# Two-phase units in the first MoE layer of a fused attention and two-MoE kernel, and a few splits on other engines

## Chip, core and metric

The kernel runs on one core of a Trainium2 chip. The metric is device time in microseconds (us), of which the median of three runs is taken. The engines of the core are named as in the profile: PE (TensorE, the matmuls), DVE (VectorE), ACT (ScalarE), POOL (GpSimd) and SP (SyncE, which issues all the DMAs here). Each engine works through its own instructions strictly in the order of the program; semaphores tie the engines together.

## What is computed

Three layers, one after the other, all in fp32:

```python
# attention, 4 batches x 8 heads, 576 positions, head size 64, block-causal mask of 64
attn = softmax(mask(q @ k.T / 8));  x = concat_heads(attn @ v)          # x: 2304 x 512
# first MoE layer (one dense expert of 2048 hidden units)
h = x @ w_in;  g = h * cos(h);  x = g @ w_out                           # 2304 x 512
# second MoE layer: 8 experts of 1024 hidden units, a gate balanced by 8 rounds
logits = x @ w_gate;  P = exp(logits - logits.max())
for _ in range(8): P /= P.sum(1); P /= P.sum(0); P *= N / E
out = sum over e of P[:, e:e+1] * (max(x @ w1[e], 0) @ w2[e])           # out: 2304 x 512
```

`w_in` and `w_out` arrive as 64-bit floats; the kernel takes the two 32-bit words of each and builds the fp32 number from them with integer operations ("conversions" below).

## The kernel before

**Split products.** A matmul takes operands of the type fp32r. To come near fp32, each operand is split into a high part (a copy into fp32r) and a low part (the operand minus its high part), and a product is three matmuls (`mm3`, L521 to L524): high by high, high by low, low by high. So for each operand some engine makes a copy (nearly always ACT) and some engine a subtraction (DVE or POOL).

**First MoE layer** (`moe1`, L710 to L916). Tokens are taken in three blocks of 768 and hidden units in 16 slices of 128. One pair of them is a unit: 48 units, `n` = 0 to 47, block by block; units 0 to 15 are called group 1 here, 16 to 31 group 2, 32 to 47 group 3. In PE's order a unit is: `hidden` for its first 384 tokens (12 matmuls), `hidden` for its other 384 tokens (12), and then `o_part` (L766) of the unit before, in two halves of 12 matmuls. `hidden` writes into one of two PSUM buffers, so a unit's first half needs the buffer that the unit before has read for the last time in `times`. Between the two lies the elementwise chain of a half: `ki` (an integer multiple of two pi, L740 on ACT or L742 on DVE), `r` (L744, DVE), the sine (L749, ACT), `times` (g = h * sine, L753, DVE), the high part of g (`g_hi`, L757, ACT), the low part (`g_lo`, L761, DVE). The weights of a unit are split as well: part 0 (`w_in`) for `hidden`, part 1 (`w_out`) for `o_part`: `w_hi` (L723, ACT) and `w_lo` (L728, POOL or DVE); `wsplit` does both and does nothing where they are there already.

In group 1, `unit` (L808) also carries the conversions of those weight tiles that attention has not converted, up to two in a unit: `magnitude` and `rounding` on ACT (L102, L109), `clamp`, `shift` and `bits` on DVE (L114, L118, L125), `add` on POOL (L131), which is issued in the unit after, and `fetch`, the load of the tile three places on (L90, SP). The order in `unit` before is: first half up to the sine, then the other half's `ki` between steps of the first, and so on: the halves alternate, and each engine's steps for the two halves are interleaved with the weights' splits and the conversions. Three split tiles are made in attention and kept in spare columns of `xh` and `xl`, so units 0 and 1 split fewer weights. In unit 1 the two halves of `hidden` are written into two of the six banks (`a11`, `a12`) that `o_part` accumulates in. Other work is hung between the units by number: `steps` (the gate's `gate_prep` L542, the gate's logits, the first expert weights), `leftover` (the end of attention, L512 to L515) and `tprep` (sums of token blocks for the second layer, one step a unit, L913).

**Second MoE layer** (L1010 to L1091). 96 groups `g` (three token blocks by 8 experts by 4 quarters of an expert) of seven products with sums of blocks in the manner of Strassen and Winograd, and six products `y` (L982) with `w2`, each added into `oa` by DVE (L1006; L1000 or L998 in the first groups). While group `g` runs, the weights of `g + 1` are prepared: the sums (`sums`, L599 to L602, POOL), high and low parts of `w1` (`hi_b` ACT, `lo_b` DVE L613 and L615) and of its sums (`hi_a` L621 ACT, `lo_a` L624 DVE, 1024 columns), and `v` for `w2` (L632 ACT, L633 POOL, twice). `open_group` of the next group needs `lo_a` at its ninth matmul. In groups 1 to 5 the gate's rounds run in between at places that `plan` (L965) names (`gate`): small products on PE and a chain of eight short steps on DVE (L956 to L959, L947 to L951).

Of the kernel before, what the change touches and what calls it, by code (L numbers as in the profile page):

```python
# [10 lines left out]
F32 = mybir.dt.float32  # L11
# [32 lines left out]
def attention_moe_kernel(ctx: ExitStack, tc: tile.TileContext, qk, v, w_a, gate, w_b, out):  # L44
# [107 lines left out]
    def attention():  # L152
        with tc.tile_pool(name="at1", bufs=1) as p1, tc.tile_pool(name="at2", bufs=2) as p2, \
# [355 lines left out]
            e = NH - 2  # L509
            n = F1 + 1  # L510
            more = [(tla[:, 0:DM], odd_sums[0][:, 0:DM]), (tt[0][:, 0:DM], RAW[1][:, 0:DM])]
# [5 lines left out]
    with tc.manual_schedule():  # L517
# [192 lines left out]
        def moe1():  # L710
            nonlocal th, tl
            with tc.tile_pool(name="m1", bufs=2) as p:
# [22 lines left out]

                def reduce_h(ps, by_act=False):
                    ki = p.tile([128, TB], I32, tag="ki", name="ki", bufs=1)
                    r = p.tile([128, TB], F32, tag="r", name="r")
                    if by_act:
                        nc.scalar.activation(ki, ps, AF.Identity, bias=quarter, scale=float(1 / TWO_PI))  # L740
                    else:
                        nc.vector.tensor_scalar(out=ki, in0=ps, scalar1=float(1 / TWO_PI), scalar2=0.25,  # L742
                                                op0=ALU.mult, op1=ALU.add)
                    nc.vector.scalar_tensor_tensor(out=r, in0=ki, scalar=float(-TWO_PI), in1=ps,  # L744
                                                   op0=ALU.mult, op1=ALU.add)
                    return r

                def sine(r):
                    nc.scalar.activation(r, r, AF.Sin, bias=half_pi)  # L749
# [42 lines left out]
                for j, unit in enumerate(FIRST):  # L792
                    wj[unit] = SPARE[j]
                last = NU - F1

                FIRST_HALF, FRAMES = NH // 4, 14
                w3 = p.tile([128, 4 * HK], F32, tag="s", name="w3", bufs=1).bitcast(I32)
                todo = list(range(FIRST_HALF, NHALF))
                share = [((n + 1) * len(todo) + FRAMES - 1) // FRAMES - (n * len(todo) + FRAMES - 1) // FRAMES
                         for n in range(FRAMES)]  # L800
                adds = []
# [6 lines left out]
                def unit(n):  # L808
                    t0 = units[n][0] * HB
                    w = wj.pop((n, 0))  # L810
                    ks = [todo.pop(0) for _ in range(share[n])] if n < FRAMES else []
                    own = [pbank.tile([128, 512], F32, tag=t, name="h")[:, 0:TB] if n == 1 else None
                           for t in ("a11", "a12")]
                    pa = hidden(*w, t0, own[0])
                    ra = reduce_h(pa, True)
                    if (n, 1) not in wj:
                        w_hi(n, 1)
                        w_lo(n, 1)
                    for k in adds:
                        conv.add(k)  # L820
                    adds[:] = ks
                    sine(ra)
                    pb = hidden(*w, t0 + TB, own[1])
                    new = (n + 1, 0) not in wj
                    if new:
                        w_hi(n + 1, 0)
                    ga = times(pa, ra)
                    if new:
                        w_lo(n + 1, 0, nc.vector)
                    rb = reduce_h(pb, True)  # L830
                    g_hi(n, 0, ga)
                    g_lo(n, 0, ga)
                    sine(rb)
                    for k in ks[0:1]:
                        conv.magnitude(k, more[k % 2][0])
                    gb = times(pb, rb)
                    g_hi(n, 1, gb)
                    g_lo(n, 1, gb)
                    for k in ks[1:2]:
                        conv.magnitude(k, more[k % 2][0])  # L840
                    for k in ks:
                        conv.rounding(k, more[k % 2][1])
                    for k in ks:
                        conv.clamp(k)
                        conv.shift(k)
                        conv.bits(k)
                        fetch(k + 3)
# [7 lines left out]
                for blk in range(N // HB - 1):  # L855
                    for i, k in ((2 if blk else 9, 2 * blk), (5 if blk else 11, 2 * blk + 1)):
                        at = (blk + 1) * F1 + i - last
                        steps.setdefault(at, []).append(lambda k=k: logits(k, psh, "h"))
                        steps.setdefault(at + 1, []).append(lambda k=k: logits_t(k, psh, "h"))
                steps[12 - last] = [gate_prep]  # L860
                tgen = None
                fetch(FIRST_HALF + 1)
                fetch(FIRST_HALF + 2)
                for n in range(NU + 1):
                    if n == F1 + 10:
                        th = post.tile([128, 3, 2, TB], F32R, tag="th", name="th", bufs=1)
                        tl = post.tile([128, 3, 2, TB], F32R, tag="tl", name="tl", bufs=1)
                        tgen = tprep(0, nc.vector)
# [5 lines left out]
                    elif n < NU:  # L874
# [5 lines left out]
                        ra = reduce_h(pa)  # L880
                        pb = hidden(*w, t0 + TB)
                        sine(ra)
                        wsplit(n + 1, 0)
# [24 lines left out]
                    if n:  # L908
# [3 lines left out]
                        wj.pop((n - 1, 1))  # L912
                    if tgen:  # L913
                        next(tgen, None)
# [38 lines left out]
        def cols(more):  # L953
# [7 lines left out]
            if more:  # L961
                rows()

        col = lambda i: lambda: cols(i < SK_ITERS - 1)
        plan = {(0, "S3"): first_logits, (0, "S4"): last_logits, (1, "A12"): gmax, (1, "y0"): start_p,  # L965
                (1, "y4"): col(0), (5, "A12"): col(SK_ITERS - 1)}
# [15 lines left out]
        def y(g, t):  # L982
# [13 lines left out]
            if tb == 0 and e == 0:  # L996
                if j == 0:
                    nc.scalar.activation(o, acc, AF.Copy)  # L998
                else:
                    nc.vector.tensor_tensor(out=o, in0=acc, in1=o, op=ALU.add)  # L1000
            elif e == 0 and j == 0:
                nc.vector.tensor_scalar(out=o, in0=acc, scalar1=p, scalar2=None, op0=ALU.mult)
            else:
                if tb == 0 and e == 1 and j == 0:
                    nc.vector.tensor_scalar(out=o, in0=o, scalar1=P[:, row, 0:1], scalar2=None, op0=ALU.mult)
                nc.vector.scalar_tensor_tensor(out=o, in0=acc, scalar=p, in1=o, op0=ALU.mult, op1=ALU.add)  # L1006
# [4 lines left out]
        for g in range(NG + 1):  # L1011
# [21 lines left out]
            def gate(at):  # L1033
                if (g, at) in plan:
                    plan[g, at]()

            if now:
# [6 lines left out]
                if g:  # L1044
                    nc.scalar.activation(c[0], x, AF.Copy)  # L1045
                    if w:
                        w.sums(fin)
                        w.hi_b()
                    product(g, x, "S2", "T2", False)
                    nc.scalar.activation(c[1], x, AF.Copy)  # L1050
                splits("T2")
                z = psz.tile([128, TB], F32, tag="z", name="hz")
# [17 lines left out]
            if now:  # L1070
# [6 lines left out]
                nc.vector.tensor_tensor(out=c[1], in0=yy, in1=c[1], op=ALU.add)  # L1077
                hidden_block(g, 1, c[1])
                wload(g + 2)
            ys(2)  # L1080
            if w and g:
                w.lo_a()
            ys(3)
            if w:
                w.v(0)
            ys(4)
            gate("y4")
            if w:
                w.v(1)
# [32 lines left out]
```

## Time and profile before

| | |
|---|---|
| median of 3 runs | 2142.88 us (2142.86 to 2143.22) |
| the profiled execution, its own time | 2142.92 us |
| its span, first to last instruction | 2141.1 us |
| PE busy | 2120.3 us (99%) |
| weight loads of PE | 1892.6 us (88%) |
| DVE busy | 1476.5 us (69%) |
| ACT busy | 979.1 us (46%) |
| POOL busy | 885.4 us (41%) |
| attention | about 0 to 189 us |
| first MoE layer | about 189 to 617 us |
| second MoE layer | about 613 to 2141 us |

Durations below come from the profiled execution. 1.82 us of its own time lie outside its span. The ends of matmuls are modelled in the profile, so that PE's idle time is shown too small; the starts are not, and lost time on PE is read here from start to start.

### The profile page before, as it was taken

Reading aid. Unit: us, or ns where it says so; the run is one execution under the profiler, and the core shown is the slowest. Engines: PE = TensorE matmul, PEld = TensorE weight load, DVE = VectorE, ACT = ScalarE, POOL = GpSimd, SP = SyncE. Lnnn points to the kernel's source line nnn. Section 1 sums busy time; section 2 is a strip of 40 time slices with the busy share of each in tenths; the row PEclk is TensorE's granted clock in tenths of the full one; section 3 lists DMA queues with packets and bytes.
Section 4 is the critical chain, followed back from the end, with each engine's and each line's share of the span. In section 5 each row is a group of like instructions: output and inputs, shape, how many; then the busy total and the mean of one; then the engine's idle time right before and its main releaser. Section 6 shows DMA issues by size and latency. Waiting matters only on the chain.

```text
span 2141.1 us, 29753 instructions
## 1 busy us (share of the span) xinstructions
PE 2120.3 (99%) x10959; PEld 1892.6 (88%) x10959; DVE 1476.5 (69%) x2409; ACT 979.1 (46%) x1846; POOL 885.4 (41%) x801
## 2 busy tenths in 40 slices
PE   9999999999999999999999999999999999999999
PEld 7887989998988888889888898888988889888898
DVE  7886886566668766666776666666777666666665
ACT  7887665344454333433443333443434433344342
POOL 4544433333323434335544343433654334343341
PEclk9999999999999999999999999999999999999999
DMA  6775320001011212112113121221212212122120
GB/s 169 184 188 141 98 72 1 7 1 40 1 40 60 79 60 71 68 60 79 60 60 109 60 79 60 71 68 60 79 60 99 69 60 79 60 71 68 60 79 30
DMA packets 77185, 152.84 MB, mean 71 GB/s; under 512 B 33232, under 2 KB 36816, under 8 KB 77040
## 3 DMA queue, kind: packets, MB, share of 16 engines
q1 hardware_dynamic: 77040, 150.95, 22.7%
q8 instruction: 86, 1.41, 0.3%
q14 instruction: 59, 0.48, 0.1%
HBM read 136.91 MB, written 4.87 MB: 66 GB/s over the span
## 4 chain that ended last, share of the span: by engine, by line
PE 84%; DVE 7%; issue 5%; POOL 2%; ACT 2%; DMA 0%; POOLq 0%; ACTq 0%; DVEq 0%
PE acc L522 12%; PE acc L524 12%; PE acc L523 12%; PE hx L524 6%; PE hx L522 6%; PE hx L523 6%; PE o L358 4%; PE acc L777 3%; PE hy L524 3%; PE hy L522 3%; PE hy L523 3%; POOL jl L728 2%; PE hz L524 2%; PE hz L523 2%; PE hz L522 2%
## 5 line engine op out<-in xcount | busy, mean ns | idle before, releaser
L633 POOL TENSOR_TENSOR wv<-stg,wv 128x512 fp32r<-128x512 f32 x190 | 333.7, 1777 | 853.9 <-ACT wv L632 853.9
L522 PE MATMUL acc<-wv,hh 128*128 128x512 f32 x1152 | 457.0, 397 | 0.0
L524 PE MATMUL acc<-wv,hl 128*128 128x512 f32 x1152 | 455.8, 396 | 0.0
L523 PE MATMUL acc<-wv,hh 128*128 128x512 f32 x1152 | 454.7, 395 | 0.0
L1006 DVE SCALAR_TENSOR_TENSOR oa<-acc,P,oa 128x512 f32<-128x512 f32 x540 | 378.9, 740 | 4.9 <-PE acc L524 4.3
L977 ACT ACTIVATE hh<-c 128x384 fp32r<-128x384 f32 x288 | 151.2, 525 | 407.1 <-DVE c L1062 167.1
L978 DVE SCALAR_TENSOR_TENSOR hl<-c,hh 128x384 fp32r<-128x384 f32 x288 | 163.9, 569 | 176.0 <-ACT hh L977 176.0
L524 PEld LDWEIGHTS acc<-wv,hl 128*128 128x128 f32 x1152 | 216.3, 188 | 53.5
L523 PEld LDWEIGHTS acc<-wv,hh 128*128 128x128 f32 x1152 | 216.1, 188 | 43.5
L522 PEld LDWEIGHTS acc<-wv,hh 128*128 128x128 f32 x1152 | 216.4, 188 | 42.6
L728 POOL TENSOR_TENSOR jl<-raw,jh 128x512 fp32r<-128x512 f32 x78 | 111.1, 1425 | 270.8 <-ACT jh L723 260.5
L1055 DVE TENSOR_TENSOR c<-hz,c 128x384 f32<-128x384 f32 x96 | 53.4, 556 | 191.2 <-PE hz L524 191.2
L1045 ACT ACTIVATE c<-hx 128x384 f32<-128x384 f32 x95 | 46.9, 493 | 275.5 <-PE hx L524 275.5
L624 DVE TENSOR_TENSOR wal<-s,wah 128x1024 fp32r<-128x1024 f32 x96 | 171.5, 1787 | 0.0
L749 ACT ACTIVATE r<-r,half_pi 128x384 f32<-128x384 f32 x96 | 59.3, 617 | 162.5 <-DVE r L744 162.2
L524 PE MATMUL hy<-xh,wal 128*128 128x384 f32 x384 | 128.9, 336 | 1.0 <-DVE wal L624 1.0
L522 PE MATMUL hx<-th,wah 128*128 128x384 f32 x384 | 128.8, 335 | 0.6 <-ACT c L1045 0.6
L522 PE MATMUL h<-xh,jh 128*128 128x384 f32 x368 | 125.0, 340 | 4.2 <-DVE g L753 4.2
L522 PE MATMUL hy<-xh,wah 128*128 128x384 f32 x384 | 128.7, 335 | 0.4 <-DVE c L1062 0.2
L524 PE MATMUL hx<-th,wal 128*128 128x384 f32 x384 | 128.6, 335 | 0.0
L523 PE MATMUL hy<-xl,wah 128*128 128x384 f32 x384 | 128.4, 334 | 0.0
L523 PE MATMUL hx<-tl,wah 128*128 128x384 f32 x384 | 128.4, 334 | 0.0
(246 smaller groups left out, 4874.2 us busy)
## 6 DMA issues: line engine op xcount, KB each, us to landing
stg<-in_w_b_dram SPq DMA_DIRECT2D x192, 512.0 KB
st<-in_qk_dram SPq DMA_DIRECT2D x64, 144.0 KB
cw<-in_w_a_dram SPq DMA_DIRECT2D x17, 512.0 KB
v<-in_v_dram SPq DMA_DIRECT2D x31, 160.0 KB
tt<-inv SPq DMA_DIRECT2D x32, 144.0 KB
out_dram<-oa SPq DMA_DIRECT2D x18, 256.0 KB
kb<-qb SPq DMA_DIRECT2D x31, 144.0 KB
qb<-qa SPq DMA_DIRECT2D x31, 144.0 KB
```

The lines of the kernel that those rows point to most:

```text
L358: nc.tensor.matmul(o[:, q0:q1], vt[:, c], e, start=c == 0, stop=True, skip_group_check=c > 0)
L522: nc.tensor.matmul(ps, lh, rh, start=first, stop=False, skip_group_check=go_on)
L523: nc.tensor.matmul(ps, lh, rl, start=False, stop=False, skip_group_check=go_on)
L524: nc.tensor.matmul(ps, ll, rh, start=False, stop=last, skip_group_check=go_on)
L624: eng.tensor_tensor(out=self.al, in0=self.s, in1=self.ah.bitcast(F32), op=ALU.subtract)
L633: eng.tensor_tensor(out=t[:, DM:2 * DM], in0=src, in1=t[:, 0:DM].bitcast(F32), op=ALU.subtract)
L728: eng.tensor_tensor(out=lo, in0=raw[units[n][1]][:, part * DM:(part + 1) * DM], in1=hi.bitcast(F32), op=ALU.subtract)
L749: nc.scalar.activation(r, r, AF.Sin, bias=half_pi)
L777: nc.tensor.matmul(acc[half, b][:, at:at + w_], w[:, s], h[:, t0:t0 + w_], start=f == 0 and i == 0 and at == 0, stop=f == F1 - 1 and i == ...
L977: nc.scalar.activation(hh, src, AF.Relu)
L978: nc.vector.scalar_tensor_tensor(out=hl, in0=src, scalar=0.0, in1=hh.bitcast(F32), op0=ALU.max, op1=ALU.subtract)
L1006: nc.vector.scalar_tensor_tensor(out=o, in0=acc, scalar=p, in1=o, op0=ALU.mult, op1=ALU.add)
```

## The change

- `unit` in group 1 becomes two-phase: both halves of `hidden` are issued, then each elementwise step for both halves, before the next step. `ki` is always made by ACT there and is written into the buffer of `r`. The conversions' steps are gathered at the end in the same manner. The low part of a unit's `w_out` (`w_lo(n, 1)`) goes from POOL to DVE; POOL keeps the `add`s.
- The conversions are shared out differently: none in unit 0, the last in unit 13 as before.
- `gate_prep` goes from unit 12 to unit 21; `leftover` and `tprep` begin one unit later; `tprep` makes no step at unit 32.
- In units 17 and 33 the next unit's weights are split ahead of the sine.
- Second layer: `lo_a` runs on POOL in groups 1 to 5 and in the last group of a token block (31 and 63); the splits of `w2` for group 1 go from group 0 into group 1; `last_logits` goes behind the last sum of group 0; the six first multiplications by `P` (L1005) go from DVE to ACT.

```diff
-            n = F1 + 1
+            n = F1 + 2
...
-                    if by_act:
-                        nc.scalar.activation(ki, ps, AF.Identity, bias=quarter, scale=float(1 / TWO_PI))
...
-                FIRST_HALF, FRAMES = NH // 4, 14
+                FIRST_HALF = NH // 4
...
+                share = [0, 2, 2, 2, 1, 2, 2, 1] + [2] * 6
...
-                    pa = hidden(*w, t0, own[0])
-                    ra = reduce_h(pa, True)
-                    if (n, 1) not in wj:
-                        w_hi(n, 1)
-                        w_lo(n, 1)
+                    one, two = (n, 1) not in wj, (n + 1, 0) not in wj
+                    hs = [hidden(*w, t0 + i * TB, own[i]) for i in range(2)]
+                    r = [p.tile([128, TB], F32, tag="r", name="r") for _ in range(2)]
+                    for a, b in zip(r, hs):
+                        nc.scalar.activation(a.bitcast(I32), b, AF.Identity, bias=quarter, scale=float(1 / TWO_PI))
                     for k in adds:
                         conv.add(k)
                     adds[:] = ks
-                    sine(ra)
-                    pb = hidden(*w, t0 + TB, own[1])
-                    new = (n + 1, 0) not in wj
-                    if new:
+                    for a, b in zip(r, hs):
+                        nc.vector.scalar_tensor_tensor(out=a, in0=a.bitcast(I32), scalar=float(-TWO_PI), in1=b,
+                                                       op0=ALU.mult, op1=ALU.add)
+                    for a in r:
+                        sine(a)
+                    if two:
                         w_hi(n + 1, 0)
-                    ga = times(pa, ra)
-                    if new:
+                    g = [times(b, a) for a, b in zip(r, hs)]
+                    if two:
                         w_lo(n + 1, 0, nc.vector)
-                    rb = reduce_h(pb, True)
-                    g_hi(n, 0, ga)
-                    g_lo(n, 0, ga)
-                    sine(rb)
-                    for k in ks[0:1]:
-                        conv.magnitude(k, more[k % 2][0])
-                    gb = times(pb, rb)
-                    g_hi(n, 1, gb)
-                    g_lo(n, 1, gb)
-                    for k in ks[1:2]:
+                    for i in range(2):
+                        g_hi(n, i, g[i])
+                    if one:
+                        w_hi(n, 1)
+                    for i in range(2):
+                        g_lo(n, i, g[i])
+                    if one:
+                        w_lo(n, 1, nc.vector)
+                    for k in ks:
                         conv.magnitude(k, more[k % 2][0])
                     for k in ks:
                         conv.rounding(k, more[k % 2][1])
                     for k in ks:
                         conv.clamp(k)
                         conv.shift(k)
+                    for k in ks:
                         conv.bits(k)
                         fetch(k + 3)
...
-                steps[12 - last] = [gate_prep]
+                steps[F1 + 5 - last] = [gate_prep]
...
-                    if n == F1 + 10:
+                    if n == F1 + 11:
...
                         pb = hidden(*w, t0 + TB)
+                        if units[n][1] == 1:
+                            wsplit(n + 1, 0)
                         sine(ra)
...
-                    if tgen:
+                    if tgen and n % F1:
                         next(tgen, None)
...
-        plan = {(0, "S3"): first_logits, (0, "S4"): last_logits, (1, "A12"): gmax, (1, "y0"): start_p,
+        plan = {(0, "S3"): first_logits, (0, "c1"): last_logits, (1, "A12"): gmax, (1, "y0"): start_p,
...
                 if tb == 0 and e == 1 and j == 0:
-                    nc.vector.tensor_scalar(out=o, in0=o, scalar1=P[:, row, 0:1], scalar2=None, op0=ALU.mult)
+                    nc.scalar.activation(o, o, AF.Copy, scale=P[:, row, 0:1])
...
                     nc.scalar.activation(c[1], x, AF.Copy)
+                    if g == 1:
+                        Weights(1).v(0)
+                        Weights(1).v(1)
...
                 hidden_block(g, 1, c[1])
+                gate("c1")
                 wload(g + 2)
...
             if w and g:
-                w.lo_a()
+                w.lo_a(nc.gpsimd if g < 6 or left == 1 else nc.vector)
             ys(3)
-            if w:
+            if w and g:
                 w.v(0)
             ys(4)
             gate("y4")
-            if w:
+            if w and g:
                 w.v(1)
```

## Rows read from the trace of the kernel before

**Rows 1.** Busy by stage: from:to, length, PE, PEld, DVE, ACT, POOL, clock, DMA, GB/s.
```profile
189.38:217.65 28.27, 24.12 (x123) 22.17 (x122) 18.42 (x32) 19.78 (x35) 10.07 (x8) 0.88 0.42 123
217.65:267.93 50.28, 50.28 (x289) 47.12 (x288) 42.20 (x70) 34.65 (x65) 23.13 (x16) 1.00 0.32 104
267.93:334.66 66.73, 61.62 (x337) 56.09 (x336) 52.33 (x88) 41.71 (x78) 23.63 (x17) 0.97 0.18 57
334.66:612.73 278.07, 276.57 (x1581) 255.13 (x1580) 180.31 (x316) 121.85 (x222) 93.48 (x66) 1.00 0.04 13
627.97:728.34 100.37, 98.25 (x490) 86.46 (x489) 80.15 (x166) 43.44 (x83) 39.68 (x38) 1.00 0.19 64
646.02:678.30 32.28, 32.28 (x165) 29.05 (x164) 26.82 (x60) 13.53 (x27) 12.72 (x13) 1.00 0.19 66
728.34:1121.34 393.00, 393.00 (x1951) 351.83 (x1950) 266.24 (x404) 159.13 (x304) 176.24 (x159) 1.00 0.21 68
1121.34:1137.70 16.36, 16.02 (x79) 14.05 (x78) 12.00 (x18) 6.25 (x12) 8.00 (x8) 1.00 0.32 111
```

**Rows 2.** What PE waited for: us in total, times, longest us.
```profile
PE h L522 <- DVE g L753: 4.2, 4, 3.1
...
PE hy L524 <- DVE wal L624: 1.0, 3, 0.3
PE h L524 <- POOL jl L728: 1.0, 2, 0.6
...
PE pcs L955 <- DVE sm L951: 0.8, 1, 0.8
PE hx L522 <- ACT c L1045: 0.6, 1, 0.6
```

**Rows 3.** PE in order of time, unit 1: start, us, line, [idle before <-releaser].
```profile
203.62 0.58 PE L777 MATMUL acc<-hh,xh 128*128 128x256 f32 x1 [3.32 <-DVE g L753]
```

**Rows 4.** ACT in order of time, unit 0: ahead of the first sine.
```profile
192.50 1.28 ACT L749 ACT_TABLE_LOAD   x1
```

**Rows 5.** DVE in order of time, a unit with two conversions.
```profile
266.14 0.56 DVE L753 TENSOR_TENSOR g<-h,r 128x384 f32<-128x384 f32 x1 [0.68 <-ACT r L749]
...
271.65 0.69 DVE L125 SCALAR_TENSOR_TENSOR raw<-w,tla 128x512 int32<-128x512 int32 x1
...
273.18 1.71 DVE L125 SCALAR_TENSOR_TENSOR raw<-cw,tt 128x512 int32<-128x512 int32 x1
...
276.04 0.56 DVE L753 TENSOR_TENSOR g<-h,r 128x384 f32<-128x384 f32 x1 [0.69 <-ACT r L749]
```

**Rows 6.** POOL in order of time, the same unit.
```profile
273.05 1.30 POOL L728 TENSOR_TENSOR jl<-raw,jh 128x512 fp32r<-128x512 f32 x1 [5.64 <-ACT jh L723]
```

**Rows 7.** SP's queue in order of time: the issue of a weight load.
```profile
221.02 0.33 SPq L90 DMA_DIRECT2D w<-in_w_a_dram  x1
```

**Rows 8.** Busy time by stage, the us in which that load has landed.
```profile
225.50:226.50 1.00, 1.00 (x8) 0.91 (x7) 0.90 (x2) 0.61 (x2) 0.01 (x1) 1.00 0.00 0
```

**Rows 9.** PE in order of time, the first matmul of unit 34.
```profile
490.79 0.41 PE L522 MATMUL h<-xh,jh 128*128 128x384 f32 x1 [0.36 <-DVE g L753]
```

**Rows 10.** DVE in order of time, a subtraction beside a POOL operation.
```profile
1028.47 2.52 DVE L70 TENSOR_TENSOR xl<-tt,xh 128x768 fp32r<-128x768 f32 x1
```

**Rows 11.** POOL in order of time, that operation.
```profile
1028.34 1.84 POOL L645 TENSOR_TENSOR tt<-xh,tt 128x768 f32<-128x768 f32 x1
```

**Rows 12.** ACT in order of time, group 3 of the experts.
```profile
670.80 1.04 ACT L621 ACTIVATE wah<-s 128x1024 fp32r<-128x1024 f32 x1
```

**Rows 13.** DVE in order of time, the same group: a round of the gate.
```profile
672.43 0.31 DVE L959 TENSOR_TENSOR P<-P,sm 128x144 f32<-128x144 f32 x1
...
673.96 0.44 DVE L951 TENSOR_REDUCE sm<-P 128x8 f32<-128x144 f32 x1
674.32 0.68 DVE L1000 TENSOR_TENSOR oa<-acc,oa 128x512 f32<-128x512 f32 x1
...
677.66 1.87 DVE L624 TENSOR_TENSOR wal<-s,wah 128x1024 fp32r<-128x1024 f32 x1
```

More of the change, by code (lines that the diff above doesn't have):

```diff
@@ L734, in wsplit, with reduce_h @@
                         w_lo(n, part)
-                def reduce_h(ps, by_act=False):
+                def reduce_h(ps):
                     ki = p.tile([128, TB], I32, tag="ki", name="ki", bufs=1)
                     r = p.tile([128, TB], F32, tag="r", name="r")
-                    if by_act:
-                        nc.scalar.activation(ki, ps, AF.Identity, bias=quarter, scale=float(1 / TWO_PI))
-                    else:
-                        nc.vector.tensor_scalar(out=ki, in0=ps, scalar1=float(1 / TWO_PI), scalar2=0.25,
-                                                op0=ALU.mult, op1=ALU.add)
+                    nc.vector.tensor_scalar(out=ki, in0=ps, scalar1=float(1 / TWO_PI), scalar2=0.25,
+                                            op0=ALU.mult, op1=ALU.add)
                     nc.vector.scalar_tensor_tensor(out=r, in0=ki, scalar=float(-TWO_PI), in1=ps,
@@ L794, in moe1 @@
                 last = NU - F1
-                FIRST_HALF, FRAMES = NH // 4, 14
+                FIRST_HALF = NH // 4
                 w3 = p.tile([128, 4 * HK], F32, tag="s", name="w3", bufs=1).bitcast(I32)
                 todo = list(range(FIRST_HALF, NHALF))
-                share = [((n + 1) * len(todo) + FRAMES - 1) // FRAMES - (n * len(todo) + FRAMES - 1) // FRAMES
-                         for n in range(FRAMES)]
+                share = [0, 2, 2, 2, 1, 2, 2, 1] + [2] * 6
                 adds = []
@@ L810, in unit @@
                     w = wj.pop((n, 0))
-                    ks = [todo.pop(0) for _ in range(share[n])] if n < FRAMES else []
+                    ks = [todo.pop(0) for _ in range(share[n])] if n < len(share) else []
                     own = [pbank.tile([128, 512], F32, tag=t, name="h")[:, 0:TB] if n == 1 else None
                            for t in ("a11", "a12")]
-                    pa = hidden(*w, t0, own[0])
-                    ra = reduce_h(pa, True)
-                    if (n, 1) not in wj:
-                        w_hi(n, 1)
-                        w_lo(n, 1)
+                    one, two = (n, 1) not in wj, (n + 1, 0) not in wj
[3 more added lines that the diff above has]
+                        nc.scalar.activation(a.bitcast(I32), b, AF.Identity, bias=quarter, scale=float(1 / TWO_PI))
                     for k in adds:
@@ L821, in unit @@
                     adds[:] = ks
-                    sine(ra)
-                    pb = hidden(*w, t0 + TB, own[1])
-                    new = (n + 1, 0) not in wj
-                    if new:
+                    for a, b in zip(r, hs):
+                        nc.vector.scalar_tensor_tensor(out=a, in0=a.bitcast(I32), scalar=float(-TWO_PI), in1=b,
+                                                       op0=ALU.mult, op1=ALU.add)
+                    for a in r:
+                        sine(a)
+                    if two:
                         w_hi(n + 1, 0)
-                    ga = times(pa, ra)
-                    if new:
+                    g = [times(b, a) for a, b in zip(r, hs)]
+                    if two:
                         w_lo(n + 1, 0, nc.vector)
-                    rb = reduce_h(pb, True)
-                    g_hi(n, 0, ga)
-                    g_lo(n, 0, ga)
-                    sine(rb)
-                    for k in ks[0:1]:
-                        conv.magnitude(k, more[k % 2][0])
-                    gb = times(pb, rb)
-                    g_hi(n, 1, gb)
-                    g_lo(n, 1, gb)
-                    for k in ks[1:2]:
+                    for i in range(2):
[7 more added lines that the diff above has]
+                    for k in ks:
                         conv.magnitude(k, more[k % 2][0])
```

## The prediction, made before the changed kernel was run

> **What bounds the kernel now.** PE. I read the stages first [rows 1]. In each row the length stands ahead of PE's busy time; where the two are equal, PE had no gap, and the first matmul of a unit or group comes at a fixed distance from the one before. From 217.65 to 267.93 six units take 50.28 us, 8.38 us each, and from 728.34 to 1121.34 25 groups of the experts take 393.00 us, 15.72 each. Nothing of the change removes a matmul, so these two lengths stay, and all that can be won is what other units and groups take beyond them. Lost time is read from start to start, as ends of matmuls are modelled.
>
> Group 1 loses most. Unit 0 starts at 189.38 and has no `o_part` ahead of it, so unit 3 is due 4.19 + 2 x 8.38 = 20.95 us later; it comes after 28.27, 7.32 too late. Units 9 to 15 (seven, 58.66 us) take 66.73, 8.07 too long. Together **15.4 us**. Groups 2 and 3 (32 units, 268.16 us) take 278.07; of the 9.9 us over, four blocks of the gate's logits take some: each has 8 products of 384 columns where a unit has 48 of about that size, so I estimate 8.38/48 x 32 = 5.6 us, and small transposes beside them. Lost are between 1.6 us (the idle time that the waits name for `jl` and for unit 34 [rows 2, 9]) and 4.3; I take **2.3**. Groups 1 to 6 of the experts take 100.37 for 94.32. Groups 2 and 3 alone (32.28) are 0.42 over each with PE busy throughout: the gate's two small products a group, so I give 2.4 of the 6.05 to such work; **about 3.6** are lost, with waits for `c`, `pcs` and `wal` [rows 2]. Group 32 takes 16.36, **0.64** over, and group 64 waits in the same way (the third of the `wal` waits). In sum about 22.5 us (1.05%) are in reach.
>
> The second view is the waits [rows 2]: the long ones are for `g`, the end of the elementwise chain; the third is the order on each engine around them.
>
> **Group 1, start.** PE waits 3.32 us in the middle of `o_part` of unit 0 [rows 3], for the banks that unit 1's `hidden` holds: that unit's `times` come late, and the clock is then at 1.2 instead of 2.4 GHz for a while (0.88 on average in this stage). The change puts no conversion into unit 0. By hand, with about 0.6 us for a step on 384 columns and its handover (the multiply itself is 0.56 [rows 5]): the second `hidden` ends at 189.4 + 4.2 = 193.6; its `ki` at 194.2; the table load that stands ahead of the first sine (1.28 [rows 4]) now comes behind this `ki`, 195.5; two sines, 196.7; then `times`, `g_hi`, `g_lo` of the second half, 198.5. PE wants it at 197.8, and its low part a third of a us later: a loss of some 0.5 to 0.9. Unit 1's chain starts behind that `g_hi`: `ki` twice, `r`, two sines and `times` need until 200.9 to 201.5; PE reaches the held banks at 198.4 + 2.1 + 0.2 = 200.7 and, the second, 1 us later. So 7.3 become about 0.8.
>
> The Trainium skill ("ScalarE: Activation LUTs", What ACT_TABLE_LOAD costs) gives 2.66 us for such a switch with its drain; the row shows 1.28 for the load, and the trace has no row for a drain there, so the two don't agree. By the page unit 0 would be 1.4 us later, and the total 1.4 us higher.
>
> **Group 1, the loop.** In a unit with two conversions the first `times` of one unit and of the next stand 9.90 us apart [rows 5]: longer than PE's 8.38, which is why PE runs dry from unit 9 on, when the lead is eaten up. Two things make it long. First, `bits` takes 0.69 us alone and 1.71 beside POOL's low part (1.30) [rows 5, 6]; likewise a DVE subtraction took 2.52 us where POOL's 1.84 us operation started 0.13 us ahead of it [rows 10, 11]: DVE stands until POOL is done. Second, the halves alternate, and DVE idles 0.68 us and more ahead of steps [rows 5].
>
> New, per unit: POOL has `add`s only, which run while DVE is at `r` and `times`, steps that read PSUM and took 0.56 beside them. DVE was busy 42.20/6 = 7.0 us a unit in units 3 to 8 [rows 1] with 10 conversions in six units; a second conversion in every unit is a third of one more, three steps of 0.69 at most: I take 0.5; the second low part, moved here, adds 0.7 (as many columns and operands as `bits` alone); the 1.0 that `bits` waited for POOL goes. That is 7.2, or 8.2 if the wait stays: under 8.38. ACT has 34.65/6 = 5.8, with the conversions' difference 6.3. From the end of the second `hidden`, `ki`, `r` and two sines and `times` take 4 steps of 0.6 for the first half: PE needs that 4.2 us later for the next `hidden`, so 1.8 us of cover; the next unit's low weights come a step later with 1.2 of cover. If that cover is gone, each us late is a us lost, in each unit. DVE's 7.2 with some 0.6 of waiting for the first sine are over ahead of the next unit's second `hidden`. So I take no loss in the loop; and `gate_prep`, which lies ahead of unit 14's wait of 3.1 [rows 2], is at unit 21, where DVE is idle for over 2 us a unit (180.31 busy of 278.07 [rows 1], a third idle). Gain of group 1: 15.4 - 0.8 = **14.6**, with ends 8 and 15.
>
> `fetch` moves behind both `bits`. A load of 512 KB issued at 221.02 had landed by 225.50 [rows 7, 8], 4.5 us; it is wanted about 5.5 us after its new issue. Behind SP's wait stand only further loads of this kind.
>
> **Groups 2 and 3.** The earlier split in units 17 and 33, the later `leftover` and the step of `tprep` left out take about 0.95 to 1.3 us from ahead of the steps that PE waited for in units 18 and 34 [rows 9]. I take 2.2 of 2.3, with ends 0 and 3. What moves by one unit meets the same third of idle DVE.
>
> **Experts.** The wait for `c` [rows 2] comes from the two splits of `w2` that ACT makes ahead of it in group 1; they go behind it and are wanted only in group 2, and `last_logits` no longer stands ahead of the sum that frees PE's buffer: 1.1 won, ends 0.6 and 1.5. In groups 31 and 63 `wal` leaves DVE, whose chain is late there with the splits of `tprep`; POOL has nothing to do at that time: 2 x 0.64 = 1.3, ends 0.6 and 1.3.
>
> In groups 2 to 5 it is less plain. `wal` (1.87 on DVE [rows 13], 1024 columns) takes on POOL about 1.84 x 1024/768 = 2.45 us [rows 11]. It starts when `hi_a` ends, 671.84 [rows 12], and the gate's round on DVE reaches its first product of two SBUF tensors at 672.43 [rows 13]: 0.6 us too late, so it stands till 674.3, and all behind it too: the reduce that PE's next small product waits for (673.96), and the add that frees an accumulator (674.32). Each then ends about 1.9 us later, 676.3 and 676.9. PE is at that product and at the sixth `y` at about 676.7 and 676.9 (the next group starts at 678.30 [rows 1], and a `y` is 15.72 us by its share of the columns, 3072 of 34560: 1.4), so it is a draw in group 3; DVE starts each round a little later than the last, so I take 0.4 in group 3, 0.7 in group 4 and 1.2 for group 5's product, 2.3 in all, against about 1.9 lost there now. **0.4 lost**, ends 3 lost and 1.9 won. For this rule the Trainium skill speaks too ("SBUF — State Buffer", SBUF: two separate sides): GpSimd and a VectorE operation with two SBUF inputs take turns for whole instructions; rows 10 and 11 agree. Were they to run side by side, the total would be 2.3 us lower. The six multiplications by `P` go to ACT, which is busy 43.44 of 100.37 us there [rows 1]; I cost them at nothing.
>
> **Sum.** 14.6 + 2.2 + 1.1 + 1.3 - 0.4 = 18.8 us. 2142.92, the profiled execution's own time and within 0.04 of the median, less 18.8 is **2124.1 us**. I say 2124.
>
> **Rivals.**
>
> *The loop stays longer than PE's 8.38 us.* DVE gets a second low part and POOL's `add`s still hold it up twice a unit. At 9.2 (8.2 from above and 1.0 of waiting) the 11 units with two conversions lose 0.8 each and the two with one win back 0.9 each, and about 1.2 us of lead is spent first: 8.8 - 1.8 - 1.2 = 5.8, so 2130. For it: busy DVE at the upper bound is at 8.2. Against: the `add`s run when DVE reads PSUM.
>
> *POOL's `wal` costs more in the gating's groups.* At its end of 3 and with a further 1 us in group 2: 2128.
>
> *Slower.* The loads land late. `fetch` comes behind both `bits`, and ACT, which stands at `magnitude`, has the next `ki` behind it. Each unit with two conversions would be longer by the landing time less 5.5 us and less the loop's spare us. It decides from about 8.5 us of landing: 11 x 2 = 22 us lost against 18.8 won, 2146. Against it: 4.5 us, and the queue is empty after it [rows 7, 8].
>
> *It does not do what it says*: the loop is ruled by something that both orders share, such as DVE's sum. Then 9 units stay at the old 9.9 and only the start, the second layer and groups 2 and 3 gain: 18.8 - 8.1 = 10.7, 2132.
>
> **Chances.** Forecast (2120.5 to 2127) 0.6, loop 0.15, POOL's `wal` 0.1, no better loop 0.08, slower 0.03, same by mishaps that I don't see 0.04. The range is 2120 to 2133: below it even all of the 22.5 us would not reach, above it are the last two. 0.2% is 4.3 us, about what can be told from no change here. Faster 0.92, same 0.05, slower 0.03.
>
> **What would show it.** Unit 0's to unit 16's start: 145.3 now, 130.7 then; a clock of 1.00 from 189 to 217; no wait of PE for `g` over 1 us; `bits` at 0.69 in all units; first `times` 8.38 apart. In groups 3 to 5 DVE's first product of a round at about 0.3 + 1.9 us, and PE waiting for `sm` by some tenths. Group 32 at 15.72. Wrong it is if PE still waits for `g` or `jl` in units 9 to 15, or if a row shows ACT waiting for a load ahead of `magnitude`.

## The result, and the profile after

The changed kernel takes **2122.98 us** (2122.82 to 2123.21, four runs), the kernel before 2142.92 beside it: a ratio of 0.9907, interval 0.989 to 0.9924, some 20 us faster. The forecast was 2124. The profiled execution took 2122.82 us, 2121.0 us of them its span.

The stages of the kernel after, cut at the same matmuls as [rows 1]; columns from:to, length, then busy time of PE, PEld, DVE, ACT and POOL, clock, DMA share, GB/s:

```profile
189.11:210.75 21.64, 21.54 (x124) 19.90 (x123) 13.78 (x28) 16.58 (x30) 4.12 (x4) 1.00 0.39 113
210.75:261.03 50.28, 50.28 (x290) 47.10 (x288) 39.84 (x79) 36.26 (x69) 13.99 (x10) 1.00 0.32 105
261.03:319.69 58.66, 58.66 (x338) 54.95 (x337) 46.70 (x94) 42.43 (x80) 17.13 (x12) 1.00 0.25 82
319.69:595.59 275.90, 275.84 (x1582) 255.20 (x1581) 180.81 (x322) 121.83 (x222) 94.95 (x66) 1.00 0.04 13
610.80:709.51 98.71, 97.57 (x489) 86.59 (x488) 74.30 (x155) 47.11 (x89) 44.12 (x39) 1.00 0.20 65
...
659.85:676.66 16.81, 16.57 (x84) 14.51 (x82) 14.49 (x31) 6.26 (x13) 7.91 (x7) 1.00 0.21 63
676.66:693.79 17.13, 16.22 (x81) 14.25 (x80) 13.70 (x30) 10.03 (x19) 8.68 (x8) 1.00 0.21 62
...
1102.51:1118.23 15.72, 15.72 (x79) 14.07 (x78) 10.88 (x18) 6.78 (x14) 7.56 (x8) 1.00 0.28 101
```

| stage | before [rows 1] | after | won | forecast |
|---|---|---|---|---|
| group 1: units 0 to 2 | 28.27 | 21.64 | 6.63 | 6.5 |
| group 1: units 3 to 8 | 50.28 | 50.28 | 0 | 0 |
| group 1: units 9 to 15 | 66.73 | 58.66 | 8.07 | 8.1 |
| groups 2 and 3 | 278.07 | 275.90 | 2.17 | 2.2 |
| experts, groups 1 to 6 | 100.37 | 98.71 | 1.66 | 0.7 |
| experts, groups 32 and 64 | 16.36 and 16.34 | 15.72 each | 1.26 | 1.3 |

These make 19.8 us of the 20.1 by which the span is shorter; 0.27 is attention, where nothing was changed (unit 0 starts at 189.11 and not at 189.38). What is to be seen in the rows: PE's busy time equals the length in units 3 to 15 and in group 32 and comes within 0.1 us of it in units 0 to 2 and in groups 2 and 3; seven units in a row take 7 x 8.38 = 58.66 us, and the clock is at 1.00 throughout.

PE's waits of after (us in total, times, longest):

```profile
PE pcs L955 <- DVE sm L951: 0.9, 1, 0.9
...
PE acc L522 <- DVE oa L1000: 0.2, 1, 0.2
```

The waits for `g`, `jl`, `wal` and the copy `c` of [rows 2] no longer stand in this list. The two shown are the gate's rounds; what else PE waits for lies in attention.

A unit with two conversions, DVE in order of time (start, us, line):

```profile
258.21 0.56 DVE L750 TENSOR_TENSOR g<-h,r 128x384 f32<-128x384 f32 x1
...
263.27 0.68 DVE L125 SCALAR_TENSOR_TENSOR raw<-cw,tla 128x512 int32<-128x512 int32 x1
263.87 0.69 DVE L125 SCALAR_TENSOR_TENSOR raw<-cw,tt 128x512 int32<-128x512 int32 x1
...
266.09 0.55 DVE L819 SCALAR_TENSOR_TENSOR r<-r,h 128x384 f32<-128x384 int32 x1 [1.07 <-ACT r L814]
266.59 0.56 DVE L750 TENSOR_TENSOR g<-h,r 128x384 f32<-128x384 f32 x1
```

The first multiplies stand 8.38 us apart (258.21, 266.59) where [rows 5] had 9.90. `bits` takes 0.69 both times, and DVE now idles 1.07 us ahead of the second `r`: it waits for ACT's `ki`, which waits for PE. The loop has become PE's.

### The profile page after: what moved, and what is told of

Its sections match the earlier page's. It is cut to its first block, busy times and chain, and to the rows that moved or that the text cites. A ratio compares the mean times of both kernels' runs of the same rounds, so it can differ in the third digit from the quotient of the medians.

```text
span 2121.0 us, 29776 instructions
## 1 busy us (share of the span) xinstructions
PE 2112.4 (100%) x10959; PEld 1888.5 (89%) x10959; DVE 1456.0 (69%) x2411; ACT 981.8 (46%) x1852; POOL 875.8 (41%) x793
## 4 chain that ended last, share of the span: by engine, by line
PE 92%; issue 4%; POOL 2%; DVE 1%; ACT 0%; DMA 0%; POOLq 0%; DVEq 0%
PE acc L522 13%; PE acc L524 13%; PE acc L523 13%; PE acc L774 7%; PE hx L524 6%; PE hx L522 6%; PE hx L523 6%; PE o L358 4%; PE hy L522 3%; PE hy L524 3%; PE hy L523 3%; PE h L522 2%; PE h L524 2%; PE h L523 2%; POOL jl L728 2%
## 5 line engine op out<-in xcount | busy, mean ns | idle before, releaser
L633 POOL TENSOR_TENSOR wv<-stg,wv 128x512 fp32r<-128x512 f32 x190 | 327.6, 1745 | 798.6 <-ACT wv L632 789.4
L728 POOL TENSOR_TENSOR jl<-raw,jh 128x512 fp32r<-128x512 f32 x63 | 92.3, 1466 | 189.5 <-ACT jh L723 169.5
L624 DVE TENSOR_TENSOR wal<-s,wah 128x1024 fp32r<-128x1024 f32 x89 | 159.7, 1794 | 0.0
L978 DVE SCALAR_TENSOR_TENSOR hl<-hx,hh 128x384 fp32r<-128x384 f32 x96 | 53.4, 557 | 104.4 <-ACT hh L977 101.7
```

The lines of the kernel that those rows point to most:

```text
L624: eng.tensor_tensor(out=self.al, in0=self.s, in1=self.ah.bitcast(F32), op=ALU.subtract)
L633: eng.tensor_tensor(out=t[:, DM:2 * DM], in0=src, in1=t[:, 0:DM].bitcast(F32), op=ALU.subtract)
L728: eng.tensor_tensor(out=lo, in0=raw[units[n][1]][:, part * DM:(part + 1) * DM], in1=hi.bitcast(F32), op=ALU.subtract)
L978: nc.vector.scalar_tensor_tensor(out=hl, in0=src, scalar=0.0, in1=hh.bitcast(F32), op0=ALU.max, op1=ALU.subtract)
```

## Experiments

All runs below stood beside runs of the kernel before at 2144.2 us on the median. That is 1.3 more than above, and much of the scatter lies in attention, which no kernel here changes: in their traces unit 0 starts anywhere between 189.0 and 191.2 us. So times are read to a us, and stages from unit 0's start on.

### The order of the steps, or the engine of the low part

The old order came back into the changed kernel, first with the low part of `w_out` on POOL, then on DVE; then the new order with the low part on POOL.

```diff
 # e1_alternating: unit(), reduce_h() and the shares of the kernel before, all else as changed
-                    hs = [hidden(*w, t0 + i * TB, own[i]) for i in range(2)]
+                    pa = hidden(*w, t0, own[0])
+                    ra = reduce_h(pa, True)
...
 # e2_alternating_low_on_dve: the same, and
-                        w_lo(n, 1)
+                        w_lo(n, 1, nc.vector)
 # e3_two_phase_low_on_pool: the changed kernel, and
-                        w_lo(n, 1, nc.vector)
+                        w_lo(n, 1)
```

> The changed kernel with the old order of group 1: the halves alternate, the low part of w_out is on POOL, and conversions are shared out from unit 0 on as before; gate_prep stays at unit 21, and the rest is as changed. Theory (the order of the steps rules the loop): the first multiplies of two units with two conversions stand about 9.9 us apart again, PE runs dry from unit 9 on, and the start loses its 7.3 us again; only what gate_prep cost (some 3 to 4 us) stays won: 2133 to 2135. Rival (gate_prep's place and the later layers did it, the order little): 2123 to 2127.

> As e1_alternating, but with the low part of w_out on DVE, so that POOL has only the adds in group 1. Theory (order): bits takes 0.7 instead of 1.7 us, but DVE gets 0.7 more and still stands between the halves, so the loop stays at 9.3 to 9.9 us and the time at 2131 to 2136. Rival (what made the loop long is that DVE waits for POOL): the loop falls under 8.38 us, and only the start's 7 us are lost: 2129 to 2131, with no wait of PE after unit 2.

> The changed kernel with the low part of w_out back on POOL. Theory (order): POOL's 1.3 us stand ahead of bits or beside clamp and shift, a two-conversion unit stays within 8.38 us, and the time is that of the changed kernel within 0.5 us: 2122.5 to 2123.5. Rival (DVE waiting for POOL): a DVE step waits a us or more in each unit, two-conversion units take 8.7 to 9.3 us, and 11 of them lose 3 to 7 us: 2126 to 2130.

Measured: 2134.2 us (ratio 0.9954, 0.9939 to 0.9969), 2136.2 (0.9963, 0.9949 to 0.9977) and 2123.2 (0.9904, 0.9889 to 0.9919). Group 1, from unit 0 to unit 16, in that order (stages as above); the kernel before took 145.28 and the changed one 130.58:

```profile
189.07:331.54 142.47, 134.51 (x747) 123.76 (x746) 110.61 (x183) 96.08 (x177) 57.22 (x41) 0.98 0.28 88
```
```profile
189.25:332.76 143.51, 135.25 (x747) 123.61 (x746) 123.14 (x198) 97.25 (x177) 33.25 (x26) 0.98 0.28 87
```
```profile
189.63:320.21 130.58, 130.49 (x747) 121.99 (x746) 103.11 (x183) 95.18 (x177) 55.34 (x41) 1.00 0.30 96
```

The new order with the low part on POOL takes exactly what the changed kernel takes; the old order with the low part on DVE takes 1.0 more than with it on POOL. So moving the low part gains nothing in either order, and the order together with the shares is worth 11.9 us of the 14.7: 7.1 in units 0 to 2 and 4.8 in units 9 to 15. The rest, 2.8, is `gate_prep`: units 13 and 14 took 12.11 and 9.89 us before and 9.43 and 9.27 in the first of these kernels, 3.3 less, while units 0 to 2 took 0.5 more there (28.75). The rows on DVE and POOL show what the move does. In the second kernel POOL has only its `add`s, and yet:

```profile
267.87 0.54 DVE L753 TENSOR_TENSOR g<-h,r 128x384 f32<-128x384 f32 x1
...
273.76 1.40 DVE L118 TENSOR_SCALAR tt<-tt 128x512 int32<-128x512 int32 x1
...
276.27 1.61 DVE L728 TENSOR_TENSOR jl<-raw,jh 128x512 fp32r<-128x512 f32 x1
277.80 0.55 DVE L753 TENSOR_TENSOR g<-h,r 128x384 f32<-128x384 f32 x1
```
```profile
273.53 1.34 POOL L131 TENSOR_TENSOR raw<-raw,rawl 128x512 int32<-128x512 int32 x1 [6.14 <-ACT ki L740]
276.03 1.29 POOL L131 TENSOR_TENSOR raw<-raw,tla 128x512 int32<-128x512 int32 x1 [1.16 <-DVE raw L125]
```

DVE still waits for POOL, now beside the two `add`s, in `shift` (1.40, elsewhere 0.43) and in the first `jl` (1.61, the second 0.67), and the multiplies are 9.93 us apart. These two waits are 1.9 us of the 9.93; without them the unit would take 8.0, by this estimate, less than PE's 8.38. So this run shows that the move leaves DVE waiting, and not that the waiting was harmless in the old order. And in the third kernel, in the new order:

```profile
258.74 0.56 DVE L750 TENSOR_TENSOR g<-h,r 128x384 f32<-128x384 f32 x1
...
261.91 1.21 DVE L114 TENSOR_SCALAR tla<-tla 128x512 f32<-128x512 f32 x1 [0.23 <-ACT tla L102]
...
267.12 0.56 DVE L750 TENSOR_TENSOR g<-h,r 128x384 f32<-128x384 f32 x1
```
```profile
261.39 1.44 POOL L728 TENSOR_TENSOR jl<-raw,jh 128x512 fp32r<-128x512 f32 x1 [4.04 <-ACT jh L723]
```

DVE waits for POOL here too (1.21 where 0.42 is usual), but in idle time that this order leaves it, and the loop is at 8.38: the new order is enough without the move.

### The start

```diff
-                share = [0, 2, 2, 2, 1, 2, 2, 1] + [2] * 6
+                share = [2, 2, 2, 1, 2, 2, 1, 2, 2, 2, 1, 2, 2, 1]
```

> The changed kernel with conversions shared out as before, two of them in unit 0. Theory: unit 1's first step on ACT stands behind four conversion steps (4 x 0.57 us by their starts), and DVE's behind six; PE waits for unit 1's multiplies in the middle of unit 0's second product, 2.3 to 3.5 us longer, and then has its clock at the lower level for some us: 2125.5 to 2128. Rival (the two-phase order alone mends the start): 2123 to 2123.7.

Measured: 2126.7 us (0.9918, 0.9903 to 0.9933). PE in order of time, and units 0 to 2 as a stage:

```profile
203.11 0.39 PE L774 MATMUL acc<-hh,xh 128*128 128x256 f32 x1 [2.34 <-DVE g L750]
```
```profile
189.23:213.46 24.23, 21.80 (x123) 19.83 (x122) 16.62 (x34) 18.84 (x34) 6.94 (x6) 1.00 0.47 144
```

24.23 against 21.64 is 2.59 us, and the wait is the one of [rows 3], 2.34 in place of 3.32. So the start's 6.6 us come in two parts, 4.0 from the order and 2.6 from keeping conversions out of unit 0. The clock did not fall, against what I expected: it stayed at 1.00 behind a wait of 2.34 us, where [rows 3] with 3.32 had 0.88 in its stage.

### The cover of the new loop

```diff
-                steps[F1 + 5 - last] = [gate_prep]
+                steps[12 - last] = [gate_prep]
```

> The changed kernel with gate_prep back at unit 12. It takes DVE 2.8 us. Theory (the new loop has a cover of 1.2 us for the next unit's low weights and of 2.3 us for the multiplies): PE loses 0.5 to 1.6 us in one unit and the clock stays up: 2123.5 to 2124.6. Rival (no cover, as in the old loop, where the units behind it lost 5.2 us): 2126 to 2128.

Measured: 2124.8 us (0.9912, 0.9897 to 0.9927). Units 13 and 14, 8.38 us each in the changed kernel:

```profile
294.82:303.27 8.45, 8.45 (x49) 7.74 (x47) 8.10 (x16) 4.87 (x10) 2.85 (x2) 1.00 0.22 63
303.27:312.17 8.90, 8.73 (x50) 7.89 (x49) 8.61 (x18) 7.69 (x15) 2.88 (x2) 1.00 0.00 0
```

0.6 us lost for 2.8 us of DVE put in its way, so about 2.2 were covered. What PE's weight loads waited for in unit 14 was `jh` (0.23 us) and `jl` (0.48): it is the cover of the next unit's weights, put at 1.2, that is about 1 us longer. The old loop lost 3.3 for the same, a part of it at the lower clock.

### The loads

```diff
-                        conv.load(k, w3 if j == 2 else conv.own[0][:, j * 2 * DM:(j + 1) * 2 * DM])
+                        for _ in range(2 if k > FIRST_HALF + 2 else 1):
+                            conv.load(k, w3 if j == 2 else conv.own[0][:, j * 2 * DM:(j + 1) * 2 * DM])
```

> The changed kernel with each load of a weight tile in group 1 issued twice into the same place, so that it lands after about 9 instead of 4.5 us. Theory: the cover of a load is about 5.5 us and the loop has 1.5 to 2 us to spare, so units with two conversions become 1.5 to 2 us longer, and with 11 of them less a first lead the time is 2133 to 2146: this is what late loads would have cost, and it says that 4.5 us is short of the point. Rival (the loads have far more cover, since SP issues them ahead of the program's order): no unit over 8.38, 2123 to 2124.

Measured: 2144.7 us, ratio 1.0004 (0.9994 to 1.0014): the whole gain is gone. SP's queue, what ACT waited for in group 1, and group 1 as a stage:

```profile
251.32 4.98 SPq L90 DMA_DIRECT2D w<-in_w_a_dram  x2
```
```profile
ACT tt L102 <- DMA w<-in_w_a_dram: 13.7, 3, 5.0
```
```profile
189.93:342.82 152.89, 139.21 (x747) 126.13 (x746) 100.49 (x198) 94.29 (x177) 35.08 (x26) 0.97 0.48 154
```

The row of SP holds two issues of 0.33 us, the second 4.65 us after the first, so a tile is there after 9 to 10 us; `magnitude` waits up to 5.0 us, and group 1 takes 152.89 us, 22.3 more than in the changed kernel. These are the late loads of the slower rival, whose price was put at 22. The sum agrees better than its parts: ten units lost 0.5 to 3.4 us each, where 11 were to lose 2, and in three stretches of 3.4 us PE's clock was at half, up to 5.1 us by my estimate (half of each stretch). In the changed kernel no `magnitude` waits for a load.

### The second layer, and POOL's `lo_a` beside the gate

```diff
 # e7_second_layer_of_before: lo_a, v, last_logits and the six multiplications as in the kernel before
-                w.lo_a(nc.gpsimd if g < 6 or left == 1 else nc.vector)
+                w.lo_a()
...
 # e9_lo_a_on_dve_beside_the_gate: the changed kernel, and
-                w.lo_a(nc.gpsimd if g < 6 or left == 1 else nc.vector)
+                w.lo_a(nc.gpsimd if left == 1 else nc.vector)
 # e6_lo_a_in_quarters: the changed kernel, and, on POOL, in lo_a
-                eng.tensor_tensor(out=self.al, in0=self.s, in1=self.ah.bitcast(F32), op=ALU.subtract)
+                for i in range(4):
+                    q = slice(i * HK, (i + 1) * HK)
+                    eng.tensor_tensor(out=self.al[:, q], in0=self.s[:, q], in1=self.ah[:, q].bitcast(F32),
+                                      op=ALU.subtract)
```

> The changed kernel with the second layer as before (lo_a on DVE everywhere, the splits of w2 for group 1 in group 0, last_logits at its old place, the six first multiplications on DVE). Theory (the parts add up): group 1 18.05 us, group 5 17.7, groups 32 and 64 16.36 again: 2.9 us more, 2125.5 to 2126.3. Rival (the gain of the second layer comes from the earlier start of the layer or is lost to something else): 2123 to 2124.5.

Measured: 2126.2 us (0.9919, 0.9905 to 0.9934). Groups 1, 5 and 32:

```profile
612.89:630.94 18.05, 17.26 (x85) 14.60 (x84) 10.16 (x26) 11.15 (x22) 6.13 (x7) 1.00 0.19 58
679.39:697.10 17.71, 16.49 (x81) 14.21 (x80) 15.30 (x32) 6.25 (x12) 7.73 (x8) 1.00 0.17 60
1106.30:1122.67 16.37, 16.02 (x80) 14.06 (x78) 12.01 (x18) 6.25 (x12) 8.01 (x8) 1.00 0.32 111
```

All three are as long as before the change, though they come 15 us sooner: the parts add up, and the first layer's gain was not lent from the second.

> The changed kernel with lo_a on DVE in groups 1 to 5, on POOL only in groups 31 and 63. Theory (on POOL it costs PE there about what it saves): groups 2 to 6 within 0.7 us of the changed kernel's, group 4 without its wait and group 5 with about 1.5 to 2 us over: 2122.6 to 2123.7. Rival (POOL's lo_a is a clear gain there): 2124 or more.

Measured: 2123.6 us (0.9906, 0.9891 to 0.992). Group 5, and groups 2 to 6:

```profile
677.47:695.10 17.63, 16.51 (x82) 14.23 (x81) 14.56 (x29) 9.02 (x17) 6.58 (x7) 1.00 0.18 60
628.97:710.82 81.85, 80.73 (x406) 71.90 (x405) 65.79 (x137) 36.29 (x70) 32.93 (x32) 1.00 0.19 65
```

Groups 2 to 6 take 81.85 us against 82.04 in the changed kernel. So in the gating's groups one long `lo_a` on POOL wins nothing over DVE: it takes from DVE in one wait what it gives back in busy time. The small gain over [rows 1], 0.47 us, is all in group 6 (16.20 us before, from 712.14 to 728.34, and 15.72 here). Of the other edits only the six multiplications lie near it: on DVE they stood from 705.5 us on, late in group 5 and into group 6, and now they are on ACT. No run takes them back alone.

> The changed kernel with POOL's lo_a as four instructions of 256 columns in place of one of 1024. Theory (DVE stands for the whole of POOL's instruction at the gate's round): the product of P that took 2.06 us takes under 1 us, the two small waits in groups 4 and 5 (0.6 and 1.1 us) go or halve: 2121.4 to 2122.4. Rival (DVE is late there by the sum of its work): no change, 2122.8 to 2123.2; or four instructions hold DVE up as often as one: 2123 to 2124.

Measured: 2121.5 us (0.9896, 0.988 to 0.9913). First group 4 of the changed kernel, DVE and POOL, and the two waits of PE there and in group 5; then DVE, POOL and groups 4 and 5 of this kernel, whose lines are shifted by three or four:

```profile
670.79 2.06 DVE L959 TENSOR_TENSOR P<-P,sm 128x144 f32<-128x144 f32 x1
```
```profile
670.29 2.39 POOL L624 TENSOR_TENSOR wal<-s,wah 128x1024 fp32r<-128x1024 f32 x1 [4.26 <-ACT wah L621]
```
```profile
675.15 0.50 PE L522 MATMUL acc<-wv,hh 128*128 128x512 f32 x1 [0.21 <-DVE oa L1000]
```
```profile
681.91 0.39 PE L955 MATMUL pcs<-sm,ones 128*128 128x8 f32 x2 [0.91 <-DVE sm L951]
```
```profile
669.87 0.39 DVE L963 TENSOR_TENSOR P<-P,sm 128x144 f32<-128x144 f32 x1
```
```profile
669.36 2.95 POOL L627 TENSOR_TENSOR wal<-s,wah 128x256 fp32r<-128x256 f32 x4 [4.97 <-ACT wah L621]
```
```profile
660.21:676.36 16.15, 16.15 (x84) 14.52 (x82) 13.23 (x32) 6.25 (x12) 8.48 (x11) 1.00 0.21 65
676.36:692.31 15.95, 15.95 (x82) 14.29 (x81) 11.88 (x27) 9.04 (x17) 7.72 (x10) 1.00 0.22 67
```

A step of 144 columns takes 0.31 us alone [rows 13] and 2.06 beside one POOL instruction of 2.39; beside four short ones it takes 0.39. Groups 4 and 5 lose 0.66 and 1.18 us less, and PE has no gap left in them. That is the mechanism that I had put at 0.7 and 1.2.

### A version that is faster than both

Three mends: `lo_a` in quarters, no step of `tprep` at unit 33 either, and a dummy sine on 128 numbers at the start of the layer.

```diff
+                early = p.tile([128, 1], F32, tag="early", name="early", bufs=1)
+                nc.scalar.activation(early, half_pi, AF.Sin)
...
-                    if tgen and n % F1:
+                    if tgen and n % F1 > 1:
```

> The changed kernel with three mends: POOL's lo_a in four instructions (as in e6_lo_a_in_quarters), a dummy sine at the start of the first layer so that the table load stands ahead of unit 0's first step, and no step of tprep at unit 33 either. Theory: the first gives 1.9 us by the lengths of groups 4 and 5, the second takes the table load's 1.28 us out of unit 0's chain and with it the 0.6 to 0.7 us that units 0 and 1 are over 12.57, the third the 0.33 us that unit 34 is over 9.75: 2120.0 to 2120.6. Rival for the second (the table load is not on the path, or unit 1's chain is late anyway): units 0 and 1 stay at 13.2 us, 2120.8 to 2121.3.

Measured: 2120.0 us (0.989, 0.9875 to 0.9905). ACT at the start, and units 0 to 2, group 1, and groups 2 and 3 as stages:

```profile
190.73 1.28 ACT L865 ACT_TABLE_LOAD   x1
192.02 0.20 ACT L865 ACTIVATE early<-half_pi 128x1 f32<-128x1 f32 x1
```
```profile
189.04:210.06 21.02, 21.02 (x123) 19.95 (x122) 13.82 (x28) 16.70 (x31) 4.13 (x4) 1.00 0.40 115
189.04:319.00 129.96, 129.96 (x747) 121.86 (x746) 100.34 (x198) 95.45 (x178) 35.34 (x26) 1.00 0.30 96
319.00:594.61 275.61, 275.61 (x1582) 254.79 (x1580) 181.54 (x322) 121.96 (x222) 93.40 (x66) 1.00 0.04 13
```

The table load now stands ahead of the first `ki`, where ACT had been idle for 0.84 us, and 0.62 of the start's 0.69 us go with it (20.95 is PE's own). From unit 0 to group 0 of the experts PE has no gap left. Another 0.3 us come from unit 34, where POOL's low part had started beside `tprep`'s step on DVE and taken 2.01 us; here it takes 1.29.

## Why the prediction was right

- *PE bounds the kernel, and a unit and a group have a fixed length*: right to 0.01 us, which is why the sum could be made by stages.
- *Start, 7.3 to 0.8*: 0.69 was left. The walk along ACT put unit 0's table load behind the second `ki`, and so it came, at 194.18 (ACT of after, first fence below). What is left are two short waits at unit 0's first `o_part`, whose weights are `hh` and then `hl` (PE's weight loads, second fence): 0.41 us for ACT's `hh` and 0.30 for DVE's `hl`, 0.71 together, where the stage's length is 0.69 above PE's own 20.95. The Trainium skill ("ScalarE: Activation LUTs", What ACT_TABLE_LOAD costs) gives 2.66 us for a table switch with its drain, 1.4 more than the load alone. Here the sine starts at the end of the load, 195.47, and so it does in the last kernel (192.02): the trace doesn't agree with the page.

```profile
194.18 1.28 ACT L746 ACT_TABLE_LOAD   x1
195.47 1.12 ACT L746 ACTIVATE r<-r,half_pi 128x384 f32<-128x384 f32 x2
```
```profile
197.79 0.30 PEld L774 LDWEIGHTS acc<-hh,xh 128*128 128x128 f32 x2 [0.41 <-ACT hh L754]
198.39 0.30 PEld L774 LDWEIGHTS acc<-hl,xh 128*128 128x128 f32 x2 [0.30 <-DVE hl L758]
```

- *Loop, no loss*: right, 50.28 and 58.66, and DVE was busy 7.04 us in the unit shown above, where 7.2 was forecast. **Of its two reasons one is shown and the other is not.** The order is shown: with the low part back on POOL, and DVE waiting for it, the new order still took 8.38. The other was that DVE's wait for POOL goes with the move of the low part, 1.0 us a unit. That step was wrong for the old order: there the `add`s that stay on POOL held DVE up by 1.9 us a unit, and group 1 came out 1.0 us longer. In the new order `bits` did come down to 0.69, as forecast, but nothing was gained by it, since the loop has room for the wait. Whether the old order would have kept up with PE if DVE had not waited for POOL at all, no run shows; the estimate of 8.0 us says that it might. The rival's two hold-ups a unit by POOL's `add`s are what the second kernel has in the old order; in the changed kernel the `add`s, at 264.10 and 265.66, fell beside `r` and `times`, which took 0.55 and 0.56 there.
- *gate_prep at unit 21 is free*: right, groups 2 and 3 show no new loss; back in group 1 it costs 0.6 in the new loop, where the cover of the weights is about 2.2 us and not 1.2.
- *Groups 2 and 3, 2.2*: 2.17. The remaining 0.33 us at unit 34 I had put at 0.1: the earlier split saved the first weights, but `tprep`'s step at unit 33 still met the second low part.
- *Experts, group 1: 1.1*: 18.05 became 16.67 by the starts of the two groups, 1.4; the ends were 0.6 and 1.5.
- *Groups 2 to 6, 0.4 lost*: 0.3 won (82.32 to 82.04, from starts 646.02, 728.34, 627.47 and 709.51). The mechanism was right and its sizes nearly so: groups 4 and 5 lost 0.66 and 1.18, of 0.7 and 1.2 forecast; group 3, which I had at 0.4, lost nothing. Had it not been for this, the change would have been 1.9 us faster. That the sum came out on the other side of zero is due to group 6, 0.48 us shorter, where the six multiplications stood that I had put at nothing.
- *Groups 32 and 64, 1.3*: 1.26.
- *The slower rival*: not what happened; `magnitude` never waits for a load. In the run with each load doubled the place was right and the price was 22.3, of 22 forecast. That it agrees so well is in part luck, since the lower clock was not in the sum.

## What to carry to other kernels

Where two halves of a step pass through two in-order engines by turns, do each step for both halves before the next: the same instructions then took 8.38 instead of 9.9 us a unit, and the engine of a single subtraction didn't matter any more. Read the worth of a stage from its length against PE's own, not from busy shares: DVE was at 42.20 of 50.28 us in units that lost nothing and at 52.33 of 66.73 in units that lost 8 [rows 1]. An instruction moved to GpSimd is better cut into short ones where DVE has a chain of small steps beside it: in groups 4 and 5 this gave 1.8 us.

## What the runs showed of the hardware beyond what was expected

- A DVE step of 0.31 us took 2.06 beside a GpSimd instruction of 2.39 us, and 0.39 beside the same work in four instructions; the four together took 2.95 us, 0.56 more.
- Beside POOL, one-input steps on DVE waited too: `clamp` took 1.21 in place of 0.42 us and `shift` 1.40 in place of 0.43.
- PE's clock stayed at 1.00 behind a wait of 2.34 us, and fell to half behind waits of 3.32 [rows 3] and 3.13 us in the kernel before. Its stretches right behind those two, as stages (the clock is the third figure from the end), come first below. The length of a single wait doesn't decide it: in the run with each load doubled the clock fell to half 1.2 us behind the end of a wait of 1.91 us (until 230.41), and again behind waits of 1.99 and 1.74 us. The first of these stretches is the last row:

```profile
203.60:210.30 6.70, 5.85 (x17) 5.08 (x18) 5.76 (x11) 4.18 (x8) 0.61 (x1) 0.50 0.37 109
316.20:319.60 3.40, 3.20 (x10) 3.09 (x11) 2.58 (x6) 2.95 (x6) 0.00 (x0) 0.50 0.00 0
```
```profile
231.60:235.00 3.40, 3.40 (x13) 3.40 (x12) 2.53 (x5) 1.69 (x4) 0.66 (x1) 0.50 0.40 126
```
